# W_o in seven products for two token blocks, two more nested down products, V in contraction halves, and a shift table over matmul groups

## The chip, the core and the metric

The kernel runs on one core of one Trainium2 chip. The metric is device time of one execution in microseconds (us), taken over repeated executions; the profiled execution has its own time, and the profile counts within its span. Engines: TensorE (PE) multiplies, with PEld its weight loads; VectorE (DVE), ScalarE (ACT) and GpSimd (POOL) work element by element; SyncE (SP), and POOL and ACT besides, issue DMAs. Each engine works through its own instructions in order and waits on semaphores.

## The reference, cut to what matters

A transformer block for 2048 tokens of width 1024: a layer norm whose scale and shift come from a conditioning vector `c`, linear attention with 32 heads, and a gated feed-forward part of inner width 3584, in bfloat16.

```python
mod = (silu(c) @ w_mod).reshape(1, 6, 1, 1024)      # sa, ca, ga, sb, cb, gb
h = layernorm(x) * (1 + ca) + sa
q, k, v = split_heads(h @ wqkv)
pq, pk = phi(q), phi(k)                             # phi(t) = where(t > 0, t + 1, exp(t)) + 1e-6
kv, z = einsum('bhsd,bhse->bhde', pk, v), pk.sum(tokens)
o = (pq @ kv) / (pq . z + 1e-6)
x = x + ga * (o @ wo)
h = layernorm(x) * (1 + cb) + sb
x = x + gb * ((gelu(h @ w_gate) * (h @ w_up)) @ w_down)
```

## The kernel before

The program first records every operation through `Plan.add` (a helper, so that nearly all VectorE additions carry line L655 and most ScalarE copies L903), then orders them: `Plan.sweep` places the operations of DVE, ACT, POOL and SP by estimated costs and due times, while TensorE keeps the order in which it was recorded; after that `Plan.refine` permutes each engine's list by the table `SHIFTS`, one number for each instruction. SP issues its loads in that order; each of eight DMA semaphores is used in turn, so the ninth load waits for the landing of the first.

Tokens are four blocks of 512 (`TG`), each of four tiles of 128; blocks 0 and 1 are group 0 and blocks 2 and 3 group 1 of the feed-forward part. In order of time:

1. `start_phase`, to 33 us. Loads the four tiles of block 0 (L648), the condition `c` and two parts of `w_mod` (L700), and the V weights (L652). The rows `c @ w_mod` are made by `row_sums` (L727), groups of four matmuls that use 32 columns of the array each and run side by side; `ModRow.columns` turns a row to columns (L718). `scale_wv` (L775) multiplies the V weights by 1 + ca, and `v_plain` (L782) makes V of block 0: 8 groups of 8 matmuls of 512 columns. `start_tile` (L767) transposes the normed tiles. After the shift `sa`, L842 writes block 0's h, and K (L1057) begins.
2. `kvq_phase` and `merge_phase`, to 188 us: V, K and Q of the other blocks in seven products instead of eight (`seven`: sums of operand halves on DVE, L958 and L1028), the kv products (L1072), and `c @ w_mod` for the other four parts (L672). `den_sums` (L1087) makes the denominators, writes their reciprocals to HBM (`den_scr`), and `den_mul` reads them back over 32 partitions (L1105) and multiplies q. `wp_step` folds kv into W_o (the result is `Wp`).
3. `wo_phase`, 188 to 245 us. `wo_tile` (L1324): for each of 16 tiles 16 matmuls of 512 columns, one addition of x on DVE, a store to `x2_scr`. For the eight tiles of group 0, `ln2_stats` takes the norm's statistics on DVE (L733, L735) and a root on ACT (L746, L747), `ln2_xhat` (L1265) normalizes, and the tile goes through HBM (L1267) to `h2_load` (L1259), a transposing DMA on SP. `h2_mod` (L1302, L1304) and `h2_sums` make the operands of the next stage.
4. `gate_up(0)` 245 to 412 us and `gate_up(1)` 492 to 657 us: 14 units of seven products (L1444), 13 of which have further nested sums (L1455, 256 columns). `wd_sums` makes sums of the down weights in group 0, on DVE, and stores them in `u_scr`; the full-size sums lie in `t_scr`.
5. `down_out(0)` and `down_out(1)`, 412 to 492 us and 657 to the end. Of the seven products, `b21`, `t0` and `b22` are `nested` (L1700: 7 x 14 matmuls of 256 columns), and `b11`, `t1`, `t2`, `t3` are `plain` (L1656: 56 matmuls of 512 columns). The plain products add up in PSUM banks 0 to 3. `sub_sums` makes the operand sums of a nested product on DVE.

Of the kernel before, what the change touches and what calls it, by code (L numbers as in the profile page):

```python
# [10 lines left out]
FP32 = mybir.dt.float32  # L11
# [8 lines left out]
SHIFTS = {  # L20
    "DVE": (
# [54 lines left out]
    ),  # L76
    "POOL": (
# [1806 lines left out]
```

## Time and profile before

| | |
|---|---|
| time, three runs | 744.41, 745.13, 745.37 us (median 745.13) |
| profiled execution | 743.69 us, of which the span is 741.9 us |
| instructions | 11731 |
| HBM read, written | 116.00 MB, 32.37 MB |
| TensorE, VectorE, ScalarE, GpSimd busy | 726.5, 626.3, 422.8, 96.7 us |

The page gives busy time and share for each engine, the span in 40 slices of 18.5 us, the DMA queues, the chain of work that ended last, and groups of instructions. Matmul durations overlap, since matmuls are pipelined: the distance between starts is what one costs in a row of them.

### The profile page before, as it was taken

The page shows a single profiled execution, that of the slowest core. Times are in us where ns is not written, and L with a number is a line of the kernel's source. Part 1 is how long each engine was busy: PE and PEld are TensorE (multiplying, and loading weights), DVE is VectorE, ACT ScalarE, POOL GpSimd, SP SyncE. Part 2 cuts the span into 40 slices and gives each one's busy share as a digit, 9 for nine tenths or more (in the row PEclk, how much of TensorE's full clock was granted, in tenths as well). Part 3 has the DMA queues.
Part 4 walks back from the last instruction along what each step waited for, and adds up shares of the span by engine and source line. Part 5 has one row for each costly group of instructions (what it writes and reads, how often), then busy time and mean ns, then how long its engine had stood idle before and what let it go on. Part 6 is the DMA issues. An engine that isn't in the chain of part 4 may idle for free.

```text
span 741.9 us, 11731 instructions
## 1 busy us (share of the span) xinstructions
PE 726.5 (98%) x4242; PEld 396.1 (53%) x4242; DVE 626.3 (84%) x1386; ACT 422.8 (57%) x772; POOL 96.7 (13%) x171
## 2 busy tenths in 40 slices
PE   4999999999999999999999999999999999999997
PEld 2444445444444455555555586545555555548664
DVE  6899978778896999999997798977788799778784
ACT  2575675769412888999867550026776767732000
POOL 1345634100031011220200000001000000000000
PEclk9999999999999999999999999999999999999999
DMA  9998798897799737565775897545231322488643
GB/s 307 330 305 227 111 185 156 312 367 236 190 282 281 249 103 228 194 215 188 260 180 168 245 284 252 204 151 188 68 114 57 115 71 100 143 232 268 205 171 101
DMA packets 141723, 149.15 MB, mean 201 GB/s; under 512 B 33760, under 2 KB 121312, under 8 KB 140384
## 3 DMA queue, kind: packets, MB, share of 16 engines
q1 hardware_dynamic: 125408, 116.14, 51.4%
q0 software_dynamic: 13904, 30.15, 14.1%
q10 hardware_dynamic: 2352, 2.10, 0.9%
q8 instruction: 33, 0.54, 0.3%
q14 instruction: 26, 0.21, 0.1%
HBM read 116.00 MB, written 32.37 MB: 200 GB/s over the span
## 4 chain that ended last, share of the span: by engine, by line
PE 85%; DVE 7%; ACT 4%; issue 2%; DMA 1%; SPq 0%; DVEq 0%; ACTq 0%
PE psum L1444 26%; PE psum L1656 13%; PE psum L1455 9%; PE psum L958 8%; PE psum L1324 7%; PE psum L1028 7%; PE psum L1700 6%; DVE mem L655 5%; PE psum L1057 4%; PE psum L782 2%; ACT mem L903 2%; PE psum L1072 1%; DMA mem<-in_w_mod_dram 1%; DVE psum L655 1%; ACT mem L1281 1%
## 5 line engine op out<-in xcount | busy, mean ns | idle before, releaser
L655 DVE TENSOR_TENSOR mem<-mem 128x512 f16<-128x512 f16 (+13 forms) x753 | 336.6, 488 | 15.2 <-ACT mem L1302 4.1
L1444 PE MATMUL psum<-mem 128*128 128x512 f16 x1144 | 282.3, 379 | 0.6 <-ACT psum L1500 0.2
L903 ACT ACTIVATE mem<-psum 128x512 f32<-128x512 f32 (+3 forms) x310 | 161.0, 550 | 112.4 <-PE psum L1700 45.5
L655 DVE TENSOR_TENSOR mem<-psum,mem 128x512 f16<-128x512 f32 (+4 forms) x204 | 155.0, 765 | 36.8 <-PE psum L1656 10.1
L1444 PEld LDWEIGHTS <-mem 128*128 128x128 f16 (+1 forms) x1144 | 111.8, 98 | 91.4 <-issue 1.6
L1455 PE MATMUL psum<-mem 128*128 128x256 f16 x742 | 115.9, 272 | 0.7 <-DVE psum L655 0.7
L1455 PEld LDWEIGHTS <-mem 128*128 128x128 f16 (+1 forms) x742 | 72.5, 98 | 55.9 <-issue 2.7
L1656 PE MATMUL psum<-mem 128*128 128x512 f16 (+2 forms) x462 | 99.2, 373 | 0.5 <-DVE mem L655 0.5
L655 DVE TENSOR_TENSOR psum<-psum,mem 128x256 f32<-128x256 f32 x106 | 45.5, 430 | 32.4 <-ACT mem L903 31.6
L1656 PEld LDWEIGHTS <-mem 128*128 128x128 f16 x462 | 45.2, 98 | 49.9 <-issue 0.7
L1700 PE MATMUL psum<-mem 128*128 128x256 f16 (+1 forms) x588 | 66.3, 273 | 0.1
L958 PE MATMUL psum<-mem 128*128 128x512 f16 (+1 forms) x280 | 62.7, 379 | 0.0
L1700 PEld LDWEIGHTS <-mem 128*128 128x128 f16 x588 | 57.5, 98 | 9.5 <-issue 0.2
L1500 ACT ACTIVATE psum<-psum 128x512 f32<-128x512 f32 x56 | 32.6, 582 | 48.4 <-PE psum L1444 28.8
L1324 PE MATMUL psum<-mem 128*128 128x512 f16 x256 | 55.9, 379 | 0.0
L1028 PE MATMUL psum<-mem 128*128 128x512 f16 x224 | 51.0, 379 | 0.0
L958 PEld LDWEIGHTS <-mem 128*128 128x128 f16 x280 | 27.0, 98 | 31.5 <-DVE mem L879 0.5
L1324 PEld LDWEIGHTS <-mem 128*128 128x128 bf16 x256 | 24.8, 98 | 30.4 <-issue 0.4
L1028 PEld LDWEIGHTS <-mem 128*128 128x128 f16 (+1 forms) x224 | 21.6, 98 | 26.7 <-issue 1.6
L1527 ACT ACTIVATE mem<-mem 128x512 f16<-128x512 f16 x56 | 34.6, 627 | 2.0 <-DVE mem L655 2.0
L1517 ACT ACTIVATE mem<-psum 128x512 f16<-128x512 f32 x56 | 33.1, 600 | 2.1 <-PE psum L1444 2.0
L733 DVE BATCH_NORM_STATS2 mem<-mem 128x6 f32<-128x512 bf16 x48 | 31.2, 676 | 1.8 <-DMA mem<-in_A_x_dram 1.7
(126 smaller groups left out, 519.5 us busy)
## 6 DMA issues: line engine op xcount, KB each, us to landing
mem<-in_B_w_gate_dram SPq DMA_DIRECT2D x14, 1024.0 KB, 5.4
mem<-in_B_w_up_dram SPq DMA_DIRECT2D x14, 1024.0 KB, 5.6
mem<-in_w_mod_dram SPq DMA_DIRECT2D x24, 512.0 KB, 6.9
mem<-us SPq DMA_DIRECT2D x24, 448.0 KB, 6.2
mem<-ts SPq DMA_DIRECT2D x6, 1792.0 KB, 7.9
mem<-in_A_x_dram SPq DMA_DIRECT2D x32, 256.0 KB, 6.4
ts<-in_B_w_down_dram POOLq DMA_DIRECT2D x28, 256.0 KB, 6.5
us<-mem POOLq DMA_DIRECT2D x7, 768.0 KB, 4.8
```

Of the source, the lines that this page charges most:

```text
L655: ve.tensor_tensor(out=out, in0=a, in1=b, op=op)
L903: ac.activation(out=t, in_=ps, func=AF.Copy)
L958: te.matmul(ps, lhsT=A[:, k, i * P:(i + 1) * P], rhs=B[:, k, :], start=(start and k == 0), stop=(k == KH - 1), skip_group_check=True)
L1028: te.matmul(o, lhsT=W[:, k, (j0 + i) * P:(j0 + i + 1) * P], rhs=h_form(a, k), start=(start and k == 0), stop=(k == KH - 1), skip_group_che ...
L1324: te.matmul(psw[:, half, :], lhsT=pqT[b][:, g, tl * P:(tl + 1) * P], rhs=Wp[:, g, half * NW:(half + 1) * NW], start=(g == 0), stop=(g == K ...
L1444: te.matmul(ps, lhsT=a[:, k, e, :], rhs=b[:, k, :], start=(start and k == 0), stop=(k == KH - 1), skip_group_check=True)
L1455: te.matmul(ps, lhsT=self.x[a][:, k, :], rhs=self.y[y][:, k, :], start=(start and k == 0), stop=(k == KH // 2 - 1), skip_group_check=True)
L1500: ac.activation(out=z, in_=x, func=AF.Copy)
L1517: ac.activation(out=o, in_=ps, func=AF.Gelu_apprx_tanh)
L1527: ac.activation(out=o, in_=o, func=AF.Gelu_apprx_tanh)
L1656: te.matmul(psm[:, q, c], lhsT=A[:, i, q * P:(q + 1) * P], rhs=wt[:, i, c], start=(start and i == 0), stop=(i == NPR - 1), skip_group_chec ...
L1700: te.matmul(ps[:, q, :], lhsT=a[:, k, q * P:(q + 1) * P], rhs=y[:, k, :], start=(start and q == 0 and k == 0), stop=(k == NPR // 2 - 1), s ...
```

## The change

W_o for blocks 2 and 3 is computed as seven products of halves (`wo_stages`, through `seven`), each of two token quarters of 128: 14 x 4 matmuls of 512 columns for each block where there were 64. DVE makes the sums: `w_sum` of `Wp` (8 of 128x1024) and `wo_sum` (4 of 128x1024 for each block); ACT copies partial products out of PSUM. The last two stages of block 3 are handed to `gate_up(0, before)` and run behind its first 8 matmuls. The statistics for the norm of group 0 move from DVE to ACT (`act_stats`).

```diff
+    def act_stats(xt, junk):
+        nmean, rstd = sum_ring(), rstd_ring()
+        ac.activation(out=junk, in_=xt, func=AF.Copy, scale=-1.0 / D, accum_out=nmean)
+        ac.activation(out=junk, in_=xt, func=AF.Square, bias=nmean, accum_out=rstd)
+        ac.activation(out=rstd, in_=rstd, func=AF.Ln, bias=eps5, scale=1.0 / D)
+        ac.activation(out=rstd, in_=rstd, func=AF.Exp, scale=-0.5)
+        return nmean, rstd
...
+    def wo_stages(b):
+        xs = {}
+        for r in range(2):
+            xs[r] = x2p_rings[b]()
...
+            sy.dma_start(out=xs[r], in_=x_in[o:o + HB, :].rearrange("(q p) n -> p q n", p=P))
...
+        def comb(ps, sb, row, col, parts=1):
+            t = wt_ring()
+            add_parts(t, ps, sb, parts)
+            tt_op(dst(row, col), t, dst(row, col), ALU.add)
+            if (row, col) == (0, 1):
+                store(0)
+
+        def direct(ps):
+            tt_op(dst(1, 0), ps, dst(1, 0), ALU.add)
+            store(1)
+        return seven(mm, comb, direct, *((QC, QD) if b == 2 else (QA, QB)), ring=wf_ring)
...
     def wo_phase(ms2):
-        for tt in range(NTT):
+        for tt in range(2 * TT):
...
-            if tt < 2 * TT:
-                ln2_xhat(tt, xt, *ln2_stats(xt, act_rstd))
+            ln2_xhat(tt, xt, *act_stats(xt, junk2))
+            if tt in (2, 3, 4):
+                for half in range(2):
+                    w_sum(Wp, WpT, (0, 1, 3)[tt - 2], half)
+            if tt == 5:
+                for j in range(4):
+                    wo_sum(2, j)
+        for half in range(2):
+            w_sum(Wp, WpT, 2, half)
+        for j in range(4):
+            wo_sum(3, j)
+        s2, s3 = wo_stages(2), wo_stages(3)
+        stages = [*s2[:5], s3[0], s2[5], s3[1], s2[6], *s3[2:5]]
...
+        return s3[5:]
```

In group 1, `b11` and `t2` become nested as well. Their weight sums are made in `gate_up(1)`, in its first seven units, by 56 additions of 128x256 on DVE, from 14 loads of 256 KB, and go to HBM in 7 stores of 512 KB. `b11`'s result is copied by ACT into PSUM banks 0 to 3 (4 copies of 128x512), where the later plain products add to it; `t2`'s result is added to the output on DVE, quarter by quarter.

```diff
+    LATER = ("b11", "t2")
...
+    def wd_later(c):
+        u, steps = wdw_ring(), []
+        for j, name in enumerate(LATER):
+            raw = wdv_rings[name]()
+            sy.dma_start(out=raw, in_=wd_full[name][:, 2 * c:2 * c + 2, :])
+            q11, q12, q21, q22 = (raw[:, e, h * HB:(h + 1) * HB] for e in range(2) for h in range(2))
+            o0, o1, o2, o3 = (u[:, j, f, :] for f in range(4))
+            steps += [(o0, q11, q12), (o2, q12, q22), (o1, o0, q22), (o3, o1, q21)]
...
+            if g and n < NPR // 2:
+                fill += wd_later(n)
...
+        if last:
+            sub_sums(A11, sub_c[:3], sub_c[3], [slice(0, 4), slice(4, NPR // 2 - 1), slice(NPR // 2 - 1, NPR // 2)])
+            run(*nested("b11", A11, sub_c[:3], sub_c[3], p1_quads))
+        else:
+            run(*plain("b11", A11, p1_out, True))
...
+            sub_sums(A21, sub_a, None, [slice(0, NPR // 2)])
+            x2, x1 = rest(1, 1), rest(1, 0, last_x)
+            n7 = nested("t2", A21, sub_a, None, c22_quads(x2, x1))
+            run(n7[0], n3[5], n7[1], n3[6], *n7[2:])
+            run(*plain("t3", A22, c21_last(x1), False))
...
+        def c22_quads(x2, x1):
+            def out(r, c, ps, sb, op):
+                t, d = f16_pair(), quad(p5v, r, c)
+                if sb is not None:
+                    tt_op(sb, ps, sb, op)
+                    ps = sb
+                tt_op(t, d, ps, ALU.subtract)
+                tt_op(d, ps, gate2(0, c), ALU.mult)
+                tt_op(t, t, gate2(1, c), ALU.mult)
+                tt_op(quad(x2, r, c), t, quad(x2, r, c), ALU.add)
...
+                tt_op(d, d, quad(x1, r, c), ALU.add)
```

At the start, the scale part of `w_mod` is loaded in quarters (two contraction halves by two column halves), and its columns come directly from matmuls of one column (`scale_cols`, 64 of them) instead of 16 matmuls of `row_sums` and a transposition; V of block 0 is split over the contraction, so that its first halves need half of the scales. The statistics of one tile move to ACT.

```diff
+    def scale_cols(h, k0, k1, ps):
+        for k in range(k0, k1):
+            for j in range(4):
+                te.matmul(ps[:, j:j + 1], lhsT=wm_ca[h][:, k, j * P:(j + 1) * P], rhs=scol[:, k:k + 1],
+                          start=(k == 0 and j == 0), stop=(k == KD - 1), skip_group_check=True)
+        if k1 == KD:
+            ve.tensor_scalar_add(out=opcA[:, 4 * h:4 * h + 4], in0=ps[:, 0:4], scalar1=1.0)
...
-    def v_plain(tl, n):
+    def v_plain(tl, n, bank, halves=(0, 1)):
+        ps = psm[:, bank, :]
+        for h in halves:
+            for k in range(h * KH, h * KH + KH):
+                te.matmul(ps, lhsT=hs0[:, k, tl * P:(tl + 1) * P], rhs=Wvs[:, k, n * NW:(n + 1) * NW],
+                          start=(k == 0), stop=(k == KD - 1), skip_group_check=True)
```

The denominators' rows in HBM get a stride of 544 elements instead of 512, so that a broadcast read is 8 rows of 1 KB for each partition where it was 8 KB in one.

```diff
-    den_scr = [scr_pool.tile([2, P // DH, 2, KH * TG], BF16, name=f"den{pr}", tag=f"den{pr}") for pr in range(2)]
+    den_scr = [scr_pool.tile([2, P // DH, KD, TG + DH], BF16, name=f"den{pr}", tag=f"den{pr}") for pr in range(2)]
```

`SHIFTS` is new for every engine and has a table for TensorE, which moves matmuls mostly in fours, eights or fourteens; in `Plan.cost` a matmul counts at least 50 (`max(n / 2.4 + 2.5, 50)`). Counted in the order that results, the matmuls of 32 array columns stand in 17 separate runs where they stood in 10 (from the first V matmul on: 17 where there were 7), and of the tail's last matmuls, 28 of 512 columns and 28 of 256 follow the last nested product.

```diff
 SHIFTS = {
+    "PE": (
+        "z1 8 28 28 28 28 4 4 4 4 4 4 4 4 4 4 4 4 4 4 4 4 4 4 4 4 8 8 8 8 8 8 8 8 8 8 8 8 8 8 8 8 -41 -41 -41 -41 21 21 "
...
+    ),
```

More of the change, by code (lines that the diff above doesn't have):

```diff
@@ new lines, in scale_cols, with x, wm, wv @@
+    def scale_cols(h, k0, k1, ps):
[5 more added lines that the diff above has]
+            ve.tensor_scalar_add(out=opcA[:, 4 * h:4 * h + 4], in0=ps[:, 0:4], scalar1=1.0)
+    def start_phase():
+        xs, order = [], []
+        def x():
+            xs.append(load_x(len(xs)))
+            order.append(plan.ops[-1])
+        def wm(h, i):
+            k = slice(i * KH, (i + 1) * KH)
+            sy.dma_start(out=wm_ca[h][:, k, :], in_=w_mod[i * KH * P:(i + 1) * KH * P, D + h * NW:D + (h + 1) * NW].rearrange(
+                "(k p) n -> p k n", p=P))
+            order.append(plan.ops[-1])
+        def wv(k, n):
+            load_w(Wv[:, k * KH:(k + 1) * KH, n * NW:(n + 1) * NW], 2 * D + n * NW, NW, k * KH, (k + 1) * KH)
+            order.append(plan.ops[-1])
+        x()
+        x()
+        wm(0, 0)
+        x()
+        wm(0, 1)
+        x()
+        wv(0, 0)
+        wv(0, 1)
+        wm(1, 0)
+        wm(1, 1)
+        wv(1, 0)
+        plan.pairs += [(c_load, order[0]), *zip(order, order[1:])]
+        wv(1, 1)
@@ L1184, in last @@
                 gp.dma_start(out=wd_full[f"t{2 * j + 1}"][:, rows, :], in_=tt[:, j])
+        return [lambda st=st: tt_op(*st, ALU.add) for st in steps[:-1]] + [last]
+    def wd_later(c):
[6 more added lines that the diff above has]
+            steps += [(o0, q11, q12), (o2, q12, q22), (o1, o0, q22), (o3, o1, q21)]
+        def last():
+            tt_op(*steps[-1], ALU.add)
+            gp.dma_start(out=v_scr[:, c], in_=u)
         return [lambda st=st: tt_op(*st, ALU.add) for st in steps[:-1]] + [last]
@@ L1367, in merge_phase, with form, mm, dst @@
         return ms2
-    AIM = (6, 10)
+    def wo_stages(b):
+        xs = {}
+        for r in range(2):
+            xs[r] = x2p_rings[b]()
+            o = b * TG + r * HB
+            plan.ahead = 36000
+            sy.dma_start(out=xs[r], in_=x_in[o:o + HB, :].rearrange("(q p) n -> p q n", p=P))
+            plan.ahead = 14000
+        def form(name):
+            lo, hi, al, be = slice(0, KH), slice(KH, KD), slice(0, HB), slice(HB, TG)
+            q, s = pqT[b], Sp[b]
+            return {"a11": q[:, lo, al], "a12": q[:, hi, al], "a22": q[:, hi, be], "s3": q[:, lo, be],
+                    "s1": s[0], "s2": s[1], "s4": s[2]}[name]
+        def mm(ps, i, a, w, start):
+            A, B = form(a), w_form(Wp, WpT, w)
+            for k in range(KH):
+                te.matmul(ps, lhsT=A[:, k, i * P:(i + 1) * P], rhs=B[:, k, :], start=(start and k == 0),
+                          stop=(k == KH - 1), skip_group_check=True)
+        def dst(row, col):
+            return xs[row][:, :, col * NW:(col + 1) * NW]
+        def store(row):
+            gp.dma_start(out=x2_scr[b][row * HB:(row + 1) * HB, :].rearrange("(q p) n -> p q n", p=P), in_=xs[row])
+        def comb(ps, sb, row, col, parts=1):
[8 more added lines that the diff above has]
+        return seven(mm, comb, direct, *((QC, QD) if b == 2 else (QA, QB)), ring=wf_ring)
+    def wo_sum(b, j):
+        lo, hi, al, be = slice(0, KH), slice(KH, KD), slice(0, HB), slice(HB, TG)
+        a11, a12, a21, a22 = (pqT[b][:, k, t] for t in (al, be) for k in (lo, hi))
+        s1, s2, s4 = Sp[b]
+        tt_op(*((s1, a21, a22, ALU.add), (s2, s1, a11, ALU.subtract), (a21, a11, a21, ALU.subtract),
+                (s4, a12, s2, ALU.subtract))[j])
+    WO_AIM = (6, 11)
     def wo_phase(ms2):
         plan.transpose = (6000, 1000000)
-        fill = [None] * NTT
-        fill[9] = h2_mods[0][0]
-        fill[11] = h2_mods[0][1]
-        fill[12] = h2_steps
-        for tt in range(NTT):
+        for tt in range(2 * TT):
             if tt == 1:
@@ L1480, with gate_up @@
     LATE, H2_AT, H2_AIM = 2, (7, 9), (9, 12)
-    def gate_up(g):
+    def gate_up(g, before=()):
         h = h2
@@ L1505, in gate_up @@
             seed(Z[e], X[e])
+        for f in before:
+            f()
         inner = None
```

182 lines of the change are left out of this document (110 added, 72 removed), and 232 rows, old and new, of tables (SHIFTS, W_AT).

## The prediction

> **What bounds the kernel now.** I read the page's busy times first, then the chain of work that ended last in order of time, then busy time by stretches (columns: us, then busy us and count for PE, PEld, DVE, ACT, POOL, then clock, DMA share, GB/s).
>
> ```profile
> PE 726.5 (98%) x4242; PEld 396.1 (53%) x4242; DVE 626.3 (84%) x1386; ACT 422.8 (57%) x772; POOL 96.7 (13%) x171
> PE   4999999999999999999999999999999999999997
> ```
>
> TensorE is busy in every slice but parts of the first and last. A busy PE need not be a fast one, so the pace is read from the chain (start, length, work):
>
> ```profile
> 155.27 0.98 PE psum L672 x16
> 156.25 1.83 PE psum L1028 x8
> 210.12 31.10 PE psum L1324 x144
> 457.73 7.64 PE psum L1700 x70
> 474.48 18.13 PE psum L1656 x84
> 492.61 1.73 PE psum L1444 x8
> 657.37 12.09 PE psum L1656 x56
> ```
>
> 144 matmuls of 512 columns in 31.10 us are 0.216 us each, 84 in 18.13 the same; 70 of 256 columns in 7.64 are 0.109. So time is matmuls times pace, except where PE waits. Sixteen matmuls of 32 array columns, four side by side, should take 4 x 0.216 = 0.86; the chain has 0.98, and the eight behind them take 1.83 where eights elsewhere take 1.73 (492.61): each separate run of such matmuls costs about 0.12 + 0.10 = 0.22 us of its own.
>
> ```profile
> 188.00:245.00 57.00, 57.00 (x279) 25.53 (x278) 48.09 (x80) 17.14 (x35) 11.50 (x21) 1.00 0.96 264
> 245.00:412.00 167.00, 165.95 (x943) 91.84 (x942) 156.39 (x401) 140.58 (x287) 21.43 (x34) 1.00 0.61 195
> 492.50:657.20 164.70, 164.44 (x947) 92.47 (x946) 132.08 (x327) 116.36 (x246) 2.84 (x4) 1.00 0.35 112
> 620.00:657.20 37.20, 37.20 (x213) 20.73 (x212) 26.60 (x63) 26.23 (x55) 0.00 (x0) 1.00 0.45 141
> 657.20:741.90 84.70, 80.81 (x533) 51.92 (x531) 62.95 (x108) 9.62 (x17) 0.00 (x0) 1.00 0.61 196
> ```
>
> W_o (first row) has no idle PE. A gate_up has 572 matmuls of 512 and 371 of 256 columns (the loops; 943 in the row): 572 x 0.2158 + 371 x 0.1092 = 163.9 us. The first takes 167.0, so PE waits some 3 us in it, the second 164.7, some 0.8. VectorE is the second bound: 156.39 of 167 us in the first gate_up.
>
> **The start.**
>
> ```profile
> 3.46 7.18 DMA mem<-in_w_mod_dram
> 14.68 1.03 PE L761 MATMUL psum<-mem 128*128 128x512 f16 x2
> 15.55 0.27 PE L718 MATMUL psum<-mem 128*128 128x2 f16 x4
> L718 PE MATMUL psum<-mem 128*128 128x2 f16 x8 | 0.5, 167 | 0.0
> 16.01 0.16 DVE mem L720
> 16.87 3.68 PE psum L782 x16
> 20.54 0.45 PE psum L767 x8
> 27.90 0.98 PE psum L727 x16
> 32.53 3.45 PE psum L1057 x16
> 35.99 0.98 PE psum L727 x16
> 16.87:33.60 16.73, 16.73 (x98) 7.55 (x98) 13.09 (x39) 8.48 (x12) 7.22 (x17) 1.00 1.07 373
> ```
>
> The second 512 KB of `w_mod` land at 3.46 + 7.18 = 10.64; afterwards the queue moves 373 GB/s, 1.41 us for each 512 KB. In the new SP order the scales of the first column half are complete at 10.64 (before, the fourth part), the first V weights at 12.05, two tiles at 13.5, the other scales at 14.9 and 16.3, V weights at 17.7, 19.1 and (behind two tiles) 21.9, the shift rows at 27.5, K weights at 30.4: the last two unmoved, since the bytes ahead are the same. A matmul of one column is in no row. Of two columns (L718), four take 0.27, of which the last alone runs 0.17: starts some 0.03 apart, the lower bound; a transpose of 128 columns is the upper, 0.45 / 8 = 0.056. I take 0.027, the nearest form. First V: 12.05 plus the 0.7 that lay between scales (16.17) and V before, some 12.7 against 16.87.
>
> From there PE does 8 V and 8 transposes (2.2) and 16 one-column matmuls to 15.3, then waits in order for the scales of 16.3: 1.0 us, with all later V behind it. Adding 56 V (12.1), 16 one-column (0.4) and the shift rows in two runs (1.3), whose data are there at 27.5, gives 30.1 with 0.1 for the columns; VectorE's path from shift to h took 32.53 - 28.88 = 3.65 before and ends at 31.5, with the second set of 16 row sums done meanwhile. Before, the same state is reached at 32.53 + 0.98 = 33.5. **Start: -2.0.** Bounds: -3.1, when only the K weights hold it; +0.5, when the first V run cold and the quarter loads are slower.
>
> The row of L761 has starts 0.4 apart, half pace, where granted clock reads 1.00. The Trainium skill ("TensorE: Matmul & The Clock Gate", Part 1) puts the warm-up at about 3.4 us of sustained work; by that estimate up to 16 V at half pace would lose 3.4 us and the sum would be 740.4 at most, less the wait that hides some. The trace agrees on two speeds, not on when.
>
> **W_o.** 16 matmuls fewer at 0.2158: **-3.45**, if VectorE keeps up:
>
> ```profile
> L655 DVE TENSOR_TENSOR mem<-psum,mem 128x1024 bf16<-128x1024 f32 x15 | 18.2, 1214 | 3.4 <-PE psum L1324 3.4
> L733 DVE BATCH_NORM_STATS2 mem<-mem 128x6 f32<-128x512 bf16 x16 | 10.2, 673 | 0.1
> L735 DVE BATCH_NORM_AGGREGATE mem<-mem 128x2 f32<-128x12 f32 x8 | 1.5, 199 | 0.1
> L655 DVE TENSOR_TENSOR mem<-mem 128x1024 bf16<-128x1024 bf16 x12 | 7.8, 683 | 0.0
> 244.94 9.10 PE L1444 MATMUL psum<-mem 128*128 128x512 f16 x40
> 247.68 1.05 ACT L1281 ACTIVATE mem<-mem 128x1024 bf16<-128x1024 bf16 x1
> 216.86 16.78 SPq L1259 DMA_TRANSPOSE mem<-xhs  x2
> 241.39 1.05 DVE L1304 TENSOR_SCALAR mem<-mem 128x512 f16<-128x512 f16 x3
> ```
>
> Removed: statistics 11.7 and eight additions 9.7. Added: 16 sums of 0.683 (10.9) and for each block three combinations of 1.2 (in two halves for one), a direct one of 1.2 and three of 0.69: 14 for both. Net +3.5 on 48.1, so 51.6 of the 53.5 us left: tight. The statistics cost ACT 16 x 1.05 plus some 6 of copies: 40 of 53, free. Two things come nearer: the second half of h2 (landed 241.39, PE at gate_up from 244.94) and the first gate weights, which stand behind both transposes on SP, whose issue held it 16.78 us. Both now wait for ACT's statistics of tile 7 (2 x 1.05 and the root) instead of VectorE's backlog; as an estimate h2 lands 2 us earlier, at 239, and PE is there at about 241, with 8 W_o matmuls (1.73) as extra cover. Behind the transposes on SP stands also the last load of x for block 3: were it late, VectorE would wait for it in order, with the first sums of gate_up behind. Bound: 0 to 3.5 (the net VectorE work if none is hidden). **I take +0.8** for this and the entry of the last down stage.
>
> **The longer list of runs.** From the first V on 17 runs of 32-column matmuls replace 7; three against two are in the start, so nine more at 0.22: **+2.0** (bounds 0, +2.0).
>
> **The down products.** 112 matmuls of 512 go, 196 of 256 come: 196 x 0.1092 - 112 x 0.2158 = **-2.76**. VectorE work:
>
> ```profile
> L655 DVE TENSOR_TENSOR mem<-mem 128x1792 f16<-128x1792 f16 x8 | 8.7, 1089 | 0.1
> L655 DVE TENSOR_TENSOR mem<-psum,mem 128x512 f16<-128x512 f32 x10 | 6.9, 689 | 8.3 <-PE psum L1656 6.4 <-ACT mem L903 1.5
> L655 DVE TENSOR_TENSOR mem<-mem,psum 128x512 f32<-128x512 f32 x4 | 2.6, 682 | 4.6 <-PE psum L1656 4.6
> L655 DVE TENSOR_TENSOR mem<-mem 128x512 f16<-128x512 f16 x17 | 7.1, 423 | 1.6 <-ACT mem L903 1.2
> L655 DVE TENSOR_TENSOR mem<-mem 128x256 f16<-128x256 bf16 x38 | 10.7, 285 | 0.2
> mem<-den SPq DMA_DIRECT2D x16, 256.0 KB, 5.5
> mem<-in_B_w_gate_dram SPq DMA_DIRECT2D x14, 1024.0 KB, 5.4
> ```
>
> The 56 weight sums (0.285, 16 us) lie in gate_up(1), where VectorE has 164.7 - 132.1 = 32 us idle: nothing; uncovered they would cost up to 16. Their 7.4 MB go where the queues move 112 GB/s. The down stage itself gets sums of A11 (5.6) and A21 (4 x 1.089), three results for `b11` (2.1), four quarters of `t2` at some 3.5 for four outputs of 1.6 (+7.6) and 0.8 at the end: +20 on 62.95, in 82 us. I cost it at nothing beyond the 0.8, as the tail's last 56 matmuls (28 x 0.2158 + 28 x 0.1092 = 9.1 us) follow the last nested product and cover its outputs. `b11`'s seven loads replace one into the same space, freed by the same units of gate_up: 0; the gate loads' 5.4 us is the order of what a late one would cost. The padded denominators (5.5 us landing, off PE's path) count 0; at most some 2 if they land twice as late.
>
> **The order by matmul groups.** PE waits 3.7 us in the two gate_ups; a permuted list can take away between all and none or add 1.5 (VectorE is full in the first). I take **-1.0**.
>
> **Sum.** 743.69 - 2.0 - 3.45 + 0.8 + 2.0 - 2.76 - 1.0 = 737.3 for the profiled execution; the median of the runs shown is 1.44 above it, so 738.7.
>
> **Rivals.**
>
> *VectorE becomes the bound of the last down stage.* 62.95 + 20.5 = 83.5 us of its work against 82 of PE; if it also idles the 10 us that the rows above show it waiting for PE, the stage lasts 93.5, 11.6 more: 750.3. It is slower than before once that idle passes some 6 us with nothing done ahead. For it: the work is real. Against: 10.6 us idle in the last 37 us of gate_up(1), where most row sums can go. 7%.
>
> *h2 and the gate weights set the start of gate_up.* Nothing moves the transposes: 3.45 lost, and VectorE's 3.5 with it in part: 742 to 745. For it: 3.5 us between landing and use; against: statistics off VectorE. 16%.
>
> *The new order does better.* All waits in gate_up go and the extra runs cost nothing: 738.7 - 2.7 - 2.0 = 734.0. Against: nothing in the rows says runs are free. 10%.
>
> *Half-width matmuls paced by their weights.* If each of 196 also waited for its load (about 0.1), 196 x 0.1 = +19.6: 758. The row of 70 in 7.64 us speaks against it. Under 1%. The Trainium skill ("TensorE: Matmul & The Clock Gate", Back-to-back issue gap) has a stream of loads and matmuls at 81 ns for 128 columns and 131 for 512, by which nesting would lose some 4.5 us (estimate, 256 columns at 98); the trace's 216 for 512 decides against it.
>
> **How the numbers follow.** The forecast (735 to 741.5) has 66%, the rivals 10, 16, 7 and 1. The likeliest is 738.7; the range 734.8 to 743 leaves out the slow rival and part of the better one. A measurement tells 0.2% (1.5 us): the forecast, the better case and most of the h2 case are faster, 0.88; 0.05 within; 0.07 slower.
>
> **What would show it.** First V near 12.7 and K near 31.5; eights behind lone fours of L792 and L1267 at 1.83; W_o's second half 24.2 us without PE idle; the last stage some 82 us long. A PE gap before gate_up, or VectorE releasing PE in the last stage, would make the sum wrong.

## The result and the profile after

| | before | after |
|---|---|---|
| median of four runs each (us) | 744.77 (744.18 to 745.37) | 738.87 (737.94 to 738.98) |
| profiled execution, its span (us) | 743.69, 741.9 | 738.87, 737.1 |
| first K matmul starts at, from there to the end (us) | 32.37, 709.53 | 32.96, 704.14 |

The kernel became 5.9 us faster by the medians (4.8 us by the profiled executions): ratio 0.9918, 95% interval 0.9901 to 0.9935. The forecast was 738.7.

The page's first part, for the kernel after, shows more instructions on every engine and TensorE still busy nearly all the time:

```profile
PE 722.0 (98%) x4353; PEld 403.0 (55%) x4353; DVE 656.4 (89%) x1469; ACT 450.5 (61%) x823; POOL 98.9 (13%) x174
```

Busy time by stretches of the kernel after (columns as in the prediction: W_o, most of gate_up(1), the rest up to the end, and the middle of W_o's second half):

```profile
187.50:241.80 54.30, 53.63 (x279) 23.55 (x276) 48.40 (x74) 41.33 (x74) 8.55 (x16) 1.00 0.87 244
488.50:657.00 168.50, 168.27 (x982) 95.74 (x980) 150.74 (x400) 114.73 (x249) 6.68 (x11) 1.00 0.49 156
657.00:737.10 80.10, 75.79 (x588) 57.21 (x585) 75.19 (x126) 12.18 (x21) 0.00 (x0) 0.99 0.77 230
217.00:232.00 15.00, 14.33 (x70) 6.37 (x69) 14.93 (x25) 9.64 (x17) 1.62 (x3) 1.00 0.83 213
```

The 54.30 us of W_o hold 53.63 of PE: gaps that were not there before. The border at 657 us is only a cut: by TensorE's new order the first down matmuls of group 1 start at 650.68 and the last of gate_up(1) at 660.69. In the 80.1 us behind it VectorE works for 75.19 (62.95 of 84.7 before). The last row has VectorE busy 14.93 of 15.00 us.

The start of the kernel after, PE and then VectorE in order of time (start, length, engine, line, operation, out<-in, form, count; in brackets the wait ahead of it):

```profile
12.48 0.61 PE L895 MATMUL psum<-mem 128*128 128x128 f16 x4 [0.67 <-DVE mem L882]
...
14.16 1.66 PE L911 MATMUL psum<-mem 128*128 128x512 f16 x4
15.66 0.61 PE L895 MATMUL psum<-mem 128*128 128x128 f16 x8
16.11 1.03 PE L911 MATMUL psum<-mem 128*128 128x512 f16 x4
...
28.86 0.40 PE L847 MATMUL psum<-mem 128*32 128x512 bf16 x4 [0.44 <-DMA mem<-in_w_mod_dram]
32.96 1.25 PE L1237 MATMUL psum<-mem 128*128 128x512 bf16 x5
12.45 0.55 DVE L978 TENSOR_SCALAR mem<-mem 128x1024 f16<-128x1024 bf16 x1
12.91 0.15 DVE L923 TENSOR_SCALAR mem<-psum 128x4 f32<-128x4 f32 x1
```

V (L911) begins at 14.16 instead of 16.87, K (L1237) only at 32.96. Between them the last shift rows (L847) wait for their load until 28.86. The first four V take 0.375 us each on average ((15.66 - 14.16) / 4). Start by start in the trace, the first three are 0.427, 0.427 and 0.427 us ahead of their followers and the fourth 0.216: half pace, then full from 15.44 on.

The chain of waits of the kernel after, its part behind the first V and its end:

```profile
18.13 10.69 DMA mem<-in_w_mod_dram
...
720.67 2.23 DVE mem L775 x4
...
734.02 0.42 DVE mem L775
```

Before, the end of the chain was TensorE's last 98 plain matmuls with three short VectorE pieces between and behind them; now it runs over VectorE's additions (L775) from 720.67 on.

### The profile page after: what moved, and what is told of

Its sections match the earlier page's. It is cut to its first block, busy times and chain, and to the rows that moved or that the text cites. A ratio compares the mean times of both kernels' runs of the same rounds, so it can differ in the third digit from the quotient of the medians.

```text
span 737.1 us, 12112 instructions
## 1 busy us (share of the span) xinstructions
PE 722.0 (98%) x4353; PEld 403.0 (55%) x4353; DVE 656.4 (89%) x1469; ACT 450.5 (61%) x823; POOL 98.9 (13%) x174
## 4 chain that ended last, share of the span: by engine, by line
PE 86%; DVE 6%; DMA 3%; ACT 2%; SPq 1%; issue 1%; DVEq 0%; ACTq 0%
PE psum L1694 31%; PE psum L1955 11%; PE psum L1705 10%; PE psum L1138 8%; PE psum L1910 7%; PE psum L1208 6%; DVE mem L775 6%; PE psum L1237 4%; PE psum L1515 3%; PE psum L1579 3%; DMA mem<-in_w_mod_dram 1%; DMA mem<-in_A_wqkv_dram 1%; PE psum L1252 1%; ACT mem L1082 1%; PE psum L792 1%
## 5 line engine op out<-in xcount | busy, mean ns | idle before, releaser
L775 DVE TENSOR_TENSOR mem<-mem 128x512 f16<-128x512 f16 (+14 forms) x857 | 377.2, 483 | 8.3 <-ACT mem L1082 1.4
L1694 PE MATMUL psum<-mem 128*128 128x512 f16 x1144 | 275.6, 379 | 0.3
L1082 ACT ACTIVATE mem<-psum 128x512 f32<-128x512 f32 (+3 forms) x320 | 168.0, 556 | 134.5 <-PE psum L1955 55.9
L775 DVE TENSOR_TENSOR mem<-psum,mem 128x512 f16<-128x512 f32 (+6 forms) x213 | 159.0, 755 | 37.9 <-ACT mem L1082 9.1
L1705 PE MATMUL psum<-mem 128*128 128x256 f16 x742 | 108.0, 272 | 0.2
L1955 PE MATMUL psum<-mem 128*128 128x256 f16 (+1 forms) x784 | 88.0, 273 | 0.0
L1955 PEld LDWEIGHTS <-mem 128*128 128x128 f16 x784 | 76.7, 98 | 11.9 <-issue 0.2
L1910 PE MATMUL psum<-mem 128*128 128x512 f16 (+2 forms) x350 | 74.8, 370 | 0.6 <-DVE mem L775 0.6
L775 DVE TENSOR_TENSOR psum<-psum,mem 128x256 f32<-128x256 f32 x106 | 44.6, 426 | 13.4 <-ACT mem L1082 10.2
L1910 PEld LDWEIGHTS <-mem 128*128 128x128 f16 x350 | 34.2, 98 | 36.9 <-issue 0.7
L1208 PE MATMUL psum<-mem 128*128 128x512 f16 x224 | 52.3, 379 | 0.0
L1138 PEld LDWEIGHTS <-mem 128*128 128x128 f16 x280 | 27.0, 98 | 32.3 <-DVE mem L775 0.9
L1208 PEld LDWEIGHTS <-mem 128*128 128x128 f16 (+1 forms) x224 | 21.1, 98 | 25.9 <-issue 2.0
L1237 PE MATMUL psum<-mem 128*128 128x512 bf16 x128 | 28.9, 379 | 0.0
L1515 PE MATMUL psum<-mem 128*128 128x512 f16 x128 | 28.3, 379 | 0.0
L1711 ACT ACTIVATE psum<-psum 128x256 f32<-128x256 f32 x53 | 20.0, 380 | 12.9 <-PE psum L1705 12.6
```

What stands on the lines that cost most here:

```text
L775: ve.tensor_tensor(out=out, in0=a, in1=b, op=op)
L1082: ac.activation(out=t, in_=ps, func=AF.Copy)
L1138: te.matmul(ps, lhsT=A[:, k, i * P:(i + 1) * P], rhs=B[:, k, :], start=(start and k == 0), stop=(k == KH - 1), skip_group_check=True)
L1208: te.matmul(o, lhsT=W[:, k, (j0 + i) * P:(j0 + i + 1) * P], rhs=h_form(a, k), start=(start and k == 0), stop=(k == KH - 1), skip_group_che ...
L1237: te.matmul(ps, lhsT=hr1[b][:, k, tl * P:(tl + 1) * P], rhs=Wk[:, k, n * NW:(n + 1) * NW], start=(k == 0), stop=(k == KD - 1))
L1515: te.matmul(psw[:, half, :], lhsT=pqT[b][:, g, tl * P:(tl + 1) * P], rhs=Wp[:, g, half * NW:(half + 1) * NW], start=(g == 0), stop=(g == K ...
```

## The experiments

In the experiments each engine's list of the kernel after is written out as a table of fixed order, so that an edit moves only what it names. Diffs are given as pieces of these lists. "K to the end" is from the first K matmul to the end of the span, which leaves the varying start out. The runs come from two chips, on which the kernel before had medians of 744.1 and of 743.6 to 744.0. No run undoes the down products, the start or the order alone; what each is worth is read from the spacing of matmuls further down.

**The kernels repeated.** No edit: the frozen list of after, and before.

> The changed kernel again, with each engine's order written out as it came from planner and tables (the same instructions in the same order). Theory A (the 1.4 us between the profiled execution of the kernel before and its median were chance, so that nothing of it belongs to a forecast): profiled execution and median within 0.5 us of each other and of 738.9. Theory B (a profiled execution lies about 1.4 us under the median whatever the kernel): the median is 1 to 1.5 us above this run's profiled execution. This run is also what the following ones are compared with.

> The kernel before, once more, for its start and for the distance from profiled execution to median. If the start differs from execution to execution in the kernel before too: K's first matmuls at 32.4 give or take 0.7 us (the second row sums 0.98 us behind them), and median and profiled execution within 1.5 us. Theory A (the median of 745.1 shown first was of the upper part of that spread): median some 744.1, profiled execution 743.5 to 744.5.

After: median 738.69 (738.21 to 739.79, five runs), ratio 0.9933 (0.9920 to 0.9945), K at 32.37, K to the end 704.03. Before: median 743.56, K at 30.95, K to the end 709.55. So the rest of the kernel repeats to about 0.1 us (704.14 and 704.03; 709.53 and 709.55), and the start does not: PE's order of time in the first execution of before, then in the repeated one:

```profile
10.68 0.62 PE L727 MATMUL psum<-mem 128*32 128x512 bf16 x4 [0.62 <-DMA mem<-in_w_mod_dram]
12.74 1.03 PE L767 MATMUL psum<-mem 128*128 128x128 f16 x8
```

```profile
10.03 0.62 PE L727 MATMUL psum<-mem 128*32 128x512 bf16 x4
12.09 0.69 PE L767 MATMUL psum<-mem 128*128 128x128 f16 x8
15.44 3.68 PE L782 MATMUL psum<-mem 128*128 128x512 f16 x16 [1.06 <-DVE mem L775]
```

The same load lands 0.65 us earlier, eight transposes take 0.69 instead of 1.03 (from the third on they start 0.056 us apart, and 0.107 in the first execution), and V comes 1.43 us earlier. The chip isn't needed for such a difference: five kernels with one and the same start (after, joined, split, gaps mended, second tail), all on one chip, had K at 32.37, 32.46, 33.92, 32.81 and 33.02. A pair of executions can't give the start's share to better than about 1.5 us.

**Runs of 32-column matmuls: joined, and split.**

```diff
 PE, kernel with joined runs (17 runs become 7)
-  L792 x4, L1208 x4, L792 x4, ...        (mod, in fours and eights)
+  L792 x12 at 151; L792 x20 at 156.5; L1267 x16 at 164.6; L792/L1267 x48 at 190
 PE, kernel with split runs (17 become 26)
-  L792 x8 | x12 | x20, ...
+  L792 x4, L1208 or L1515 x4, L792 x4, L1208 or L1515 x4, ...
```

> The changed kernel with one thing altered, TensorE's order between 148 and 196 us: the lone fours and eights of matmuls of 32 array columns (lines 792 and 1267) are put together, so that from the first V matmul on there are 7 separate runs instead of 17; nothing else moves. Theory A (each separate run costs some 0.2 us of its own): 10 runs fewer, -2.0 us against the repeated changed kernel, some 736.9. Theory B (the cost is a wait for weights or denominators that the fours only show, or they are spread because joined ones would wait): no gain, 738.9, or a wait ahead of the joined runs and up to 740.

> The reverse: the runs of eight, twelve and twenty matmuls of 32 array columns between 148 and 196 us are cut into fours by moving four of the following 512-column matmuls in between, 26 or 27 separate runs instead of 17. Theory A (0.2 us for each separate run): +2.0 us against the repeated changed kernel, some 740.9. Theory B (cutting is free): 738.9.

Joined: 736.9 (736.54 to 737.57), ratio 0.9906 (0.9893 to 0.9920), 1.8 below after; K to the end 702.34, 1.69 less for ten runs fewer, 0.17 each. Split: 744.38, ratio 1.0002, 3.5 above the 740.9 expected; K to the end 709.08, 5.05 more. PE in order of time, split runs:

```profile
190.32 0.40 PE L1267 MATMUL psum<-mem 128*32 128x512 bf16 x4
190.65 1.04 PE L1515 MATMUL psum<-mem 128*128 128x512 f16 x4
191.62 0.40 PE L792 MATMUL psum<-mem 128*32 128x512 bf16 x4
...
203.42 5.34 PE L1515 MATMUL psum<-mem 128*128 128x512 f16 x24 [1.23 <-DVE mem L775]
209.86 2.32 PE L1515 MATMUL psum<-mem 128*128 128x512 f16 x10 [1.10 <-DVE mem L775]
```

Four narrow matmuls hold 0.33 us (190.65 - 190.32) where four side by side at full pace would be 0.216, and the four wide ones behind them 0.97 where four are 0.863: 0.11 at each side, 0.22 a run. Nine more runs make 2.0 of the 5.05. The 1.23 and 1.10 are waits for VectorE's additions of x, which free the PSUM banks (the first ends at 203.37, PE goes on at 203.42), and a wait on ScalarE's copies (L1178) adds 0.4: 4.7 in all. VectorE was late because, in its own order, a copy of the split sums of `c @ w_mod` stood ahead. The waits from 195 to 206 us, split runs (what waited, for what: us in total, times, longest):

```profile
DVE mem L798 <- PE psum L792: 3.5, 1, 3.5
```

So the price of a run is 0.17 to 0.22 us, and what the split kernel loses beyond it is a result that comes late to an engine with other work behind it.

The Trainium skill ("TensorEngine Tiling (Array Packing)", Key Properties) says that changing the tiling mode drains TensorE, and gives no price; the trace agrees, with 0.11 us at each change.

**The two gaps in W_o.** After, PE waits twice in the second half. PE and ScalarE of the kernel after:

```profile
219.95 2.75 PE L1579 MATMUL psum<-mem 128*128 128x512 f16 x12 [0.17 <-DVE mem L805]
...
222.03 0.20 ACT L875 ACTIVATE mem<-mem 128x1 f32<-128x1 f32 x1
222.13 1.00 ACT L1082 ACTIVATE mem<-psum 128x1024 f32<-128x1024 f32 x1
223.19 1.02 PE L1579 MATMUL psum<-mem 128*128 128x512 f16 x4 [0.49 <-ACT mem L1082]
```

The copy (L1082) that frees PE's banks stands behind the last tile's statistics and root (L873, L875).

```diff
 ACT
-  L873, L875 (last tile), L1082
+  L1082, L873, L875 (last tile)
 PE
-  L1579 group 2, L1579 first product of block 2
+  L1579 first product of block 2, L1579 group 2
 DVE
-  L775 (other), L775 (next product's operand), ..., L1457 (last tile), L775 x2
+  L775 (next product's operand), L775 (other), ..., L775 x2, L1457 (last tile)
```

> The changed kernel with five operations moved in W_o: TensorE runs the four matmuls that complete block 2's first product (start 220.8 in the profile) ahead of another group; ScalarE copies that product (line 1082) ahead of the last tile's statistics instead of behind them; VectorE makes the operand that the next product needs one place earlier, and normalizes the last tile two places later. Theory A (TensorE's two gaps of 0.33 and 0.66 us at 219.4 and 222.3 come from this order alone, and gate_up follows W_o without waiting): -0.8 to -1.0 us against the repeated changed kernel, some 738.0, and no gap inside line 1579. Theory B (h2, which is now about 1 us later, or the gate weights set the start of gate_up): the gaps go, but gate_up starts where it did, 738.9.

738.95, K to the end 703.89: 0.14 less than r_after, and the 112 matmuls of the seven products took 25.02 us instead of 25.20. Both gaps are gone; two others, of 0.18 us each, stand in their place (at 229.41 and 230.61). PE in order of time and one stretch, gaps mended:

```profile
218.58 10.65 PE L1579 MATMUL psum<-mem 128*128 128x512 f16 x48
229.41 1.02 PE L1579 MATMUL psum<-mem 128*128 128x512 f16 x4 [0.18 <-DVE mem L775]
...
```

```profile
217.00:232.00 15.00, 14.65 (x71) 6.51 (x70) 14.83 (x26) 10.49 (x19) 1.62 (x3) 1.00 0.74 185
```

The new waits name VectorE, which is busy 14.83 of 15.00 us. Neither theory as written was right. The rows point at VectorE's backlog as what paces W_o's second half, with the gap at whichever of its readers comes last; this is argued and not shown, for the next run, which was to relieve VectorE, doesn't bear it out.

**Block 3 of W_o plain again.** Block 3's operand sums and combinations are left out; its tiles go as in the first half.

```diff
-        s2, s3 = wo_stages(2), wo_stages(3)
+        s2, s3 = wo_stages(2), [lambda tt=tt: wo_tile(tt, psC) for tt in (12, 13, 14, 15)]
-            wo_sum(3, j)
```

> The changed kernel with W_o of block 3 plain again: 64 matmuls of 512 columns instead of 56, four additions of 128x1024 on VectorE (1.2 us each) in place of the four sums of q and the seven combinations (some 12 us in all); block 2 and everything else as they are, in the same order. Theory A (TensorE sets the pace of W_o, and each block's eight matmuls fewer are worth 8 x 0.216): +1.7 us against the repeated changed kernel, some 740.4. Theory B (VectorE, busy nearly all of the time there, is the bound, and seven products only move the limit): with some 7 us of its work gone the waits of W_o go too, and the time is 738.7 or less.

Median 750.05, profiled 746.2 with a span of 744.4. It should have relieved VectorE; instead PE waited more. The waits by line between 187 and 400 us (what waited, for what: us in total, times, longest), the kernel with block 3 plain:

```profile
PE psum L1703 <- DVE psum L775: 3.1, 1, 3.1
```

The theory that the waits vanish once VectorE has less to do fell. Against the repeated kernel, K to the end is 7.9 us longer, by the spacing of starts 3.3 in W_o (1.73 of them the eight more matmuls, the rest longer waits) and 4.8 in the gate_ups. There VectorE stood for the landing of a store of weight sums (`us`), and TensorE behind it. VectorE and PE in order of time, then a stretch, block 3 plain:

```profile
374.13 0.43 DVE L775 TENSOR_TENSOR mem<-mem 128x512 f16<-128x512 bf16 x1 [4.12 <-DMA us<-mem]
375.33 3.12 PE L1692 MATMUL psum<-mem 128*128 128x512 f16 x8
374.00:378.00 4.00, 3.05 (x9) 1.23 (x9) 3.83 (x14) 0.98 (x2) 0.00 (x0) 0.57 0.96 288
```

The eight matmuls behind the wait are 0.37 us apart ((378.28 - 375.33) / 8, since PE's next group starts at 378.28) instead of 0.216, with a granted clock of 0.57: the wait of 3.1 us costs TensorE some 1.2 more behind it. Why the store landed late is open. So it is no clean undo, and it doesn't price the seven products alone. Its other five executions are 2.9 to 5.1 us above the profiled one, and their granted clocks are 0.995 to 0.997 where after has 0.999 to 1.000; more waits of this kind would fit, but these executions have no trace.

**The start: scales first.**

```diff
 DVE
-  L898, L882, L978, L923, L903 x4, L898
+  L898, L923, L882, L903 x4, L898, L978
 PE
-  transposes of tiles 3, 2, then the first V halves
+  the first V halves, then the transposes of tiles 3, 2
```

> The changed kernel with the order of the start altered, nothing else. VectorE finishes the first half of the scales (line 923) ahead of the last two tiles' normalizations (lines 882, 978) instead of behind them, and scales the first V weights between the two; TensorE runs the first two groups of V (tiles 0 and 1) ahead of the transposes of tiles 2 and 3; four of the last V matmuls move ahead of the last four row sums, which wait for the shift rows of w_mod. Theory A (the first V is late because the scales stand behind the normalizations on VectorE, and what it gains reaches K because V work fills the wait for the shift rows): first V at some 12.8 instead of 13.8 to 14.2 us, K at 31.4 to 32.0 instead of 32.4 to 33.0, -0.9 us, some 737.8. Theory B (the landing of the shift rows, 28.8 in the profile, sets K, whatever comes ahead of it): TensorE only waits longer ahead of the row sums, K where it was, 738.7.

738.95; the scales (L923) were done at 11.77 instead of 12.91, the first V at 13.08. PE in order of time, scales first:

```profile
13.08 3.32 PE L911 MATMUL psum<-mem 128*128 128x512 f16 x8
...
32.73 0.39 PE L1237 MATMUL psum<-mem 128*128 128x512 bf16 x1
33.75 2.54 PE L1237 MATMUL psum<-mem 128*128 128x512 bf16 x11 [0.64 <-DVE mem L1021]
```

Eight V took 0.395 us each ((16.24 - 13.08) / 8; 0.427 in the middle, 0.217 for the last), and K then waited 0.64 for VectorE's h. K to the end is 705.07, 1.0 more than in the repeated kernel. A V that starts earlier starts slow, and what it gains is waited for at the end of the start.

**The start: a warm TensorE.** Five idle matmuls are added in the gaps behind `start_tile`; their result is not used.

```diff
     start_tile(halves[1], 1, xh[1])
+    keep_warm(5, NW)
```

> The changed kernel with five idle matmuls of 512 columns (the kernel's own keep_warm) added on TensorE in the first 12.5 us, three behind the second transposes and two behind the second sixteen one-column matmuls, where it waits otherwise; nothing else moves. Theory A (the first V matmuls start 0.39 us apart instead of 0.216 because TensorE stood idle for most of the first 12 us; before the change the row sums of 512 columns kept it busy there): the first four V take 0.9 instead of 1.5 us. What this gives to K depends on the shift rows of w_mod: if their landing (28.8) sets K, K stays within 0.3 us of 32.4 to 33.0 and the time at 738.7; if the late V does, K comes 0.7 us earlier, some 738.0. Theory B (the pace has another cause, the operands or the banks): still 0.39 us apart.

PE in order of time, idle matmuls added:

```profile
13.73 1.33 PE L911 MATMUL psum<-mem 128*128 128x512 f16 x4
14.90 0.61 PE L895 MATMUL psum<-mem 128*128 128x128 f16 x8
...
29.02 0.40 PE L847 MATMUL psum<-mem 128*32 128x512 bf16 x4 [0.66 <-DMA mem<-in_w_mod_dram]
```

The first four V take 1.17 us instead of 1.50. Start by start, the second comes 0.525 behind the first, and the next ones 0.215 apart: full pace, so the half pace was TensorE's own and goes away when it has worked before. The time didn't move: 738.5, K at 33.13. The shift rows wait longer for their load (0.66 instead of 0.44) and start at 29.02, and K follows 4.1 us behind, as in after (28.86 and 32.96). In the repeated kernel PE shows no wait there (order of time):

```profile
27.83 0.83 PE L847 MATMUL psum<-mem 128*32 128x512 bf16 x12
```

The last four of these start at 28.27, though, 0.07 us behind their load's landing (17.71 + 10.49), and K at 32.37. So in these three executions the landing sets K. It isn't the only limit: in the second tail kernel below, with the same start, V begins at 14.55, TensorE comes to the last shift rows at 28.92, 0.80 us after they landed, and K at 33.02. V's work and the landing end within a microsecond of each other.

**The padded denominators.**

```diff
-    den_scr = [... [2, P // DH, KD, TG + DH] ...]
+    den_scr = [... [2, P // DH, KD, TG] ...]
```

> The changed kernel with the denominators' rows in HBM unpadded again (a stride of 512 elements instead of 544), all else the same. Theory A (the padding lies off TensorE's path): 738.7, no difference, with the reads landing some 5.5 us after their issue instead of 4.2. Theory B (a later landing reaches TensorE through the multiplications of q that W_o waits for): up to +2 us, with a wait of TensorE at lines 1515 or 1579.

738.68, K to the end 704.05, no wait of PE changed. The view of the tile of the denominators, without the padding and then in before:

```profile
DMA to landing us min/median/max: 3.3/4.2/6.4
```

```profile
DMA to landing us min/median/max: 3.9/5.5/8.9
```

Without the padding too the reads land sooner than in before (in after it was 4.2 as well), so padding isn't the cause; what is stays open.

**The tail, twice.** With joined runs, the last quarter's first half (14 matmuls of 256 columns) is put ahead of PE's last 14 full-width ones; in the other kernel VectorE's additions are reordered as well, to read that half sooner.

```diff
 PE
-  L1910 x14 (512, quarter 1), L1910 x14 (256), L1910 x14 (256)
+  L1910 x14 (256), L1910 x14 (512, quarter 1), L1910 x14 (256)
 DVE (second kernel only; PE's order as in the first)
-  L775 x2 (other), L775 x3, L775 (last quarter's first half)
+  L775 x2, L775 (last quarter's first half), L775 x2 (other), L775
```

> The joined runs of 32-column matmuls together with a swap in TensorE's last matmuls: the first half of the last token quarter (14 matmuls of 256 columns) runs ahead of a full quarter (14 of 512) instead of right before its own second half, which writes the same PSUM bank that VectorE still reads. Theory A (the 0.7 us that TensorE waits at 730.9 is that bank): -1.8 for the runs and -0.6 for the swap, some 736.3. Theory B (the end is set by VectorE's backlog and the last store, whatever TensorE's order): as with the joined runs alone, 736.9.

> The joined runs and the swap in TensorE's last matmuls again (start as in the changed kernel, no idle matmuls), with three VectorE operations moved: two additions and the read of the last quarter's first half, which releases the PSUM bank, stand ahead of two other additions instead of behind them. The swap alone left TensorE waiting 0.74 us at 728.4 as before, since VectorE came to that read only at 728.9, behind five additions. Theory A (VectorE's order in the last 10 us is that wait): no wait of TensorE at line 1910, and -0.5 us from K's start to the end against the joined runs (702.3 us there), some 736.4. Theory B (VectorE's work itself, not its order, ends last): the wait goes, but the end stays where it was after K's start, 702.3 us, some 736.9.

737.25 and 736.97, K to the end 702.18 and 702.38, beside 736.9 and 702.34 with the joined runs alone. Order of time, first kernel and then second:

```profile
725.88 3.07 DVE L775 TENSOR_TENSOR mem<-mem 128x512 f32<-128x512 f32 x5
728.87 0.42 DVE L775 TENSOR_TENSOR mem<-psum,mem 128x256 f16<-128x256 f32 x1
729.34 1.69 PE L1910 MATMUL psum<-mem 128*128 128x256 f16 x14 [0.58 <-DVE mem L775]
```

```profile
721.76 9.05 PE L1910 MATMUL psum<-mem 128*128 128x512 f16 x55
```

In the first the wait stays, since VectorE gets to the read only behind five other additions. In the second it is gone, 55 matmuls run through, and the end doesn't move: against the joined runs alone the down products take 0.8 us less on PE, and from the start of the last matmul to the end it is 4.89 us instead of 3.95. VectorE's work ends last in both. (Before, too, PE waited 0.52 us for VectorE ahead of its last 14 matmuls.)

**All together.** Joined runs, tail, scales first and idle matmuls in one kernel.

> Put together: joined runs of 32-column matmuls, the swap in the last matmuls, the altered order of the start (scales first on VectorE, first V ahead of the transposes, four V ahead of the last row sums) and the five idle matmuls. Theory A (with TensorE at full pace the earlier V counts, since V work also fills the wait for the shift rows): first eight V in 1.8 us instead of 3.3 (altered order alone), K at 31.5 to 32.2, 736.9 - 0.7 for the start, some 736.2. Theory B (the shift rows' landing, and VectorE's path from them to h, set K): K at 32.4 to 33.0 all the same, 736.9.

737.03 (ratio 0.9905, 0.9891 to 0.9919), no better than the joined runs alone. PE in order of time:

```profile
11.92 2.19 PE L911 MATMUL psum<-mem 128*128 128x512 f16 x8
...
31.52 0.39 PE L1238 MATMUL psum<-mem 128*128 128x512 bf16 x1
32.55 3.62 PE L1238 MATMUL psum<-mem 128*128 128x512 bf16 x16 [0.64 <-DVE mem L1022]
```

V starts at 11.92, at full pace behind a first gap of 0.52, and K at 31.52, as the prediction had it. But K then stands 0.64 us for VectorE's h, and K to the end is 703.28, 0.94 more than with the joined runs alone. TensorE came to the last shift rows at 28.27, 0.43 us after they landed, with four V put ahead of them. Joining the runs is the version that beats both kernels.

## Why the prediction was right, and where it was not

The terms behind the start, from spacing of matmul starts summed by line (first execution of each kernel; before had its second shift rows, 0.98 us, behind the first K, and they are taken out):

| term (us) | predicted | measured |
|---|---|---|
| W_o, 256 matmuls in 55.37 to 240 in 53.15; tail behind the last matmul's start 3.65 to 3.94 | -3.45 + 0.8 | -2.22 + 0.29 |
| narrow matmuls of 148 to 196 us and the wide ones of L1028 (then L1208) among them, 54.65 to 56.15 | +2.0 | +1.50 |
| down products, 161.72 to 159.02 | -2.76 | -2.70 |
| the two gate_ups, 331.59 to 330.61 | -1.0 | -0.98 |
| K, kv and the rest, 101.57 to 101.26 | 0 | -0.31 |
| sum | -4.41 | -4.42 |

In the repeated pair the measured terms are -2.21 + 0.28, +1.50, -2.67, -0.89 and -0.58. That the sum is met to 0.01 us is luck: W_o with the tail came out 0.72 worse than forecast, the runs 0.50 and the rest 0.31 better.

**W_o.** The step "W_o's second half 24.2 us without PE idle" failed: PE waited twice there and lost 1.0 us in all, 0.33 at 219.4 and 0.66 at 222.3 by the spacing, so it took 25.20. "51.6 of the 53.5 us left: tight" was too high for VectorE over the whole stage (48.40 of 54.30), but in the middle of the second half it is full (14.93 of 15.00). The 0.8 was meant for this stage and the entry of the last down stage: W_o alone fell 1.23 short of its -3.45. The h2 rival didn't come: PE goes on to gate_up at 241.79 without a wait.

**Runs.** Predicted were 0.22 each; measured are 0.17 each when ten are taken away or nine come with the change (1.50 / 9), and 0.22 around a single run by its spacing. The rival in which they are free fell; joining them is worth 1.8 us.

**Down products and VectorE behind them.** The matmul arithmetic came in whole, with the 784 half-width matmuls in 85.81 us, 0.109 each; the rival of weight-paced halves is gone. The slow rival had the mechanism right in part, for the end of the chain does run over VectorE, and the size wrong: the tail grew by 0.29, not by 11.6. Its condition was that VectorE goes on idling for PE, and that is what failed. VectorE's longest waits from 657 us to the end, before and then after (what waited, for what: us in total, times, longest):

```profile
DVE mem L655 <- PE psum L1656: 13.5, 6, 5.6
```

```profile
DVE mem L775 <- ACT mem L1082: 0.4, 1, 0.4
```

With such waits gone VectorE does 12.2 us more work there (the forecast had 20) in 4.6 us less. Part went ahead: VectorE's work in gate_up(1) grew to 150.74 of 168.50 us (132.08 of 164.70 before), and the first down matmuls start inside it. Which part of this the new order gave isn't shown.

**The order by groups.** gate_up lost 0.98 us of waiting, as taken. The permutation couldn't be tried alone, as it belongs to the other engines' lists; the size agrees, the cause isn't shown.

**The start.** Here the prediction failed. Its step "First V: 12.05 plus the 0.7 that lay between scales (16.17) and V before, some 12.7" and the path to "Start: -2.0" had K at 31.5; measured were 14.16 and 32.96, so -0.4 in the first pair of executions (33.35 to 32.96, with the 0.98 above) and +0.4 in the repeated one (31.93 to 32.37). Two things were missed. VectorE normalized another tile (L978, 0.55 us) ahead of the scales, in its own order, and TensorE ran at half pace until 15.44. Removing them takes V to 11.92, and the whole gains nothing that can be measured. What failed at the end of the start is the term "the shift rows at 27.5": they landed at 28.82 (18.13 + 10.69), and K followed 4.1 us behind. The bytes ahead are the same, as the prediction says, but they moved more slowly (0 to 26.4 us, before and then after):

```profile
0.00:26.40 26.40, 16.32 (x98) 7.86 (x99) 20.11 (x69) 7.65 (x17) 6.81 (x30) 1.00 0.95 329
```

```profile
0.00:26.40 26.40, 17.18 (x149) 9.47 (x150) 18.98 (x66) 10.94 (x22) 7.51 (x32) 1.00 0.97 322
```

329 against 322 GB/s (333 and 325 in the repeated pair) are, as an estimate, 0.6 us of the 1.3. Also, the loads up to the shift rows are 8.39 MB, and 9.34 MB had come through their queue when they landed: later loads move alongside, and the step counted only those ahead. Why the rate fell is open; the first 36 us hold 6452 packets under 2 KB where before had 4528, but no run tests that, and none moves the shift rows' loads ahead of block 1's tiles.

The bound for half pace in the prediction is wrong in its sum: 738.7 and 3.4 are 742.1, not 740.4. Three V at half pace cost 0.6 us in after.

**From the profiled execution to the median.** "The median of the runs shown is 1.44 above it" was carried over to the kernel after, where it is 0.0 and, repeated, 0.5 (738.21 and 738.69). Before, too, the offset was 1.2 in the repeated run (742.33 and 743.56), not 1.44; starts alone differ by more than that between executions (32.37 and 30.95). So 738.7 met 738.87 by luck: two errors of about 1.5 us, a start too fast and an offset too large, cancel; the profiled time, 737.3, was 0.9 to 1.6 below what came.

## What to carry to other kernels

Where TensorE sets the time, count matmuls by the pace that the trace has for their width, and then count each change of array width: a run of narrow matmuls costs about 0.2 us however short, so put narrow work together. Before adding new work on an engine to its present idle time, look at what it waits for: here most of VectorE's waits in the last stage shrank. A load that stays in its place can go on setting the end of a stage, and starting that stage's other work earlier then only moves the wait. And do not carry the gap between one execution and a median over to another kernel.

## What was not expected of the hardware

TensorE ran at half pace in the first microseconds while the granted clock read 1.00. Stretch of the kernel after:

```profile
12.80:16.10 3.30, 3.30 (x24) 2.08 (x23) 3.27 (x10) 0.61 (x2) 0.00 (x0) 1.00 1.10 350
```

Single starts show the pace: 0.427 us at 512 columns up to 15.44, 0.216 from there, 3.0 us after TensorE's last idle (12.48). With scales first the change came at about 15.8. With the same five idle matmuls it came at about 13.0 in one kernel and at 10.7 in the other, so the amount of work ahead doesn't fix the moment alone. The Trainium skill ("TensorE: Matmul & The Clock Gate", Part 1) gives about 3.4 us of sustained work for the warm-up and a spacing of 426.7 ns cold and 215.7 warm at 512 columns; the trace agrees on the spacing with 0.427 and 0.216. The column for the granted clock doesn't show the slow start (1.00), though it does show the slow matmuls behind the 3.1 us wait with block 3 plain (0.57).

Between executions of one and the same program the first 33 us differed by 1.4 us (first V of before at 16.87 and 15.44), while the 700 us behind them agreed to 0.1.
